# The last transform step of batches 1 to 7: table as weights on 64x32 parts, data streamed, blocks transposed by VectorE

## The chip, the cores and the metric

The kernel runs on one core of a Trainium2 chip. The metric is device time in microseconds (us) for one execution. All times before the change are of this one core; three runs were timed, and one more execution was recorded by the hardware profiler.

The engines are named as in the profile: PE is TensorE (matmuls), PEld its weight loads, DVE is VectorE, ACT is ScalarE, POOL is GpSimd, SP is SyncE (it only issues DMAs here). A matmul takes its weights (`lhsT`) from SBUF, streams the other operand (`rhs`) through the array, and writes a bank of PSUM; there are eight banks. A float32 matmul stands in the trace as two matmul records, with two weight loads.

## The reference

```
x: (8, 3008, 256)                       # batch, sequence, channels
X = rfft(x, axis=1)
y = irfft(X * (filt_r + 1j * filt_i), n=3008, axis=1)
t = y.reshape(24064, 256)
g = t @ w_gate                          # 256 x 1536
out = (g * sigmoid(g) * (t @ w_val)) @ w_out
```

A filter in the frequency domain along the sequence, then a SwiGLU block on every token. Everything is float32.

## The kernel before

The transform of length 3008 = 47 x 64 is done as matrix products with tables of sines and cosines, in steps of length 47 and 64, and the step back as the last of them. The SwiGLU block is done by a scheme with fewer products than the plain one (sums of blocks of inputs and of weights, then products of the sums), with its hidden blocks 0 to 3 and pairs of them.

**Order of the work.** The loop over batches `b` (lines 1431 to 1541) has 12 steps per batch. A step is a `Group(b, k, g)`: one chunk `k` of the tokens (4 chunks of 8 x 94 tokens) and one third `g` of the hidden dimension (`NG = 3`). Each step walks the hand-written list `SCHEDULE` (lines 88 to 96), in which each token stands for one instruction, or a few, on one engine; the order on every engine is this order. `pin` keeps it. A prime on a token means the group before the one it would normally be for. The tokens that matter here:

- `P`, `Q`, `A`, `B`, `E` (`product`, line 1116): two matmuls of 128x128 weights on 188 columns, four records, into a bank.
- `f`, `D`, `c`, `x`, `s`, `y`, `e`, `m`, `l` (`step`, line 1126): copies and sums on ACT, DVE and POOL that fill banks for the products (`s` for `A`, `e` for `E`) or take them out. `g`, `u`: Silu on ACT. `h`, `v`: DVE products into the hidden tiles `h`. `S`: sums of hidden blocks on POOL.
- `W`, `o`, `z`, `x0.o` to `x5.o` (`project`, line 1184): projection matmuls of 376 columns for the group before, their sum into the output tile `o` (line 1234 on DVE; line 1232 on ACT for the first third), the transpose of 32x32 blocks in `o` by DVE (line 1191, only after the last third), and the output DMAs on SP (line 1205). `LAST` (lines 99 to 102) is the order after the last group.
- `b0` to `b7`: pieces of the next batch's transform, `quads` (steps 0 to 3, line 733) and `fours` (steps 4 to 10, line 813). Their matmuls already run on parts of the array, `quads` on 32x32 parts, `fours` on 64x64 parts.
- `t0.0` to `t4.3`: pieces of the last transform step. `plan[step]` (lines 1434 to 1468) lists up to five pieces; `tN.m` advances piece `N`.
- `n1` to `n3`: sums for the next chunk (`combine_sequence`, line 1062).

**The last transform step.** `stage3(k, step)` (line 1008) makes the tile `y` of a chunk from the two halves `t4[k, 0]` and `t4[k, 1]`, each with 2 x 48 rows for each of four row groups `n`. `y` has eight parts of 188 tokens: 0 to 3 from channels 0 to 127 and 4 to 7 from channels 128 to 255, the latter with a multiple (`KS` = -1, 0, 1, 2) of the former taken off. For batch 0 it uses the table `wi_t`. For later batches 4 x 96 rows are packed into three tiles of 128 rows each (`BACK`, lines 120 to 123, loaded by four DMAs, lines 687 to 692); each step is three matmuls with data as weights and the table `back_t` streamed (141, 188 and 141 columns), and the result lands in the order of `y` with tokens of the two tables in turn, written to every second element of the bank (lines 1021 to 1027). Steps with `cb == 0` are taken out by one ACT copy of 376 (line 1041); steps with `cb == 1` by two operations of 188 (lines 1049 to 1054), DVE or ACT, that also take off the multiple.

For batch b its pieces stand so: chunk 1 in steps 0 (t2, t4) and 1 (t1, t3), chunk 2 in step 4 (t0 to t3), chunk 3 in step 7 (t1 to t4), chunk 0 of the next batch in step 11 (t0 to t3). `t4` is loaded two pieces per chunk: for chunks 1, 2, 3 in steps 0, 2 and 5, at the start and at `B01`; for chunk 0 of the next batch in step 10, at `A12` and `E23`.

**Banks.** One bank is in a pool of its own (`fps`, line 240) for `stage1`, `stage2a`, `stage2b` and `stage3`; the other seven (`NB = 7`, line 68) are in the pool `wps` for all else. A tile that is asked for gets a bank whose last readers are done.

Of the kernel before, what the change touches and what calls it, by code (L numbers as in the profile page):

```python
# [66 lines left out]
TQ = TH // 2  # L67
NB = 7

# [29 lines left out]
LAST = """  # L99
S00 S01 W1 S20 S21 S10 S11 W5 o1 W2 o5 S30 S31 W6 o2 z0.o o6 W3 o3 z1.o x0.o x1.o x2.o x3.o x4.o  # L100
x5.o W7 q4 o7 z3.o W4 o4 z2.o X0.o X1.o X2.o X3.o X4.o X5.o
""".split()
# [9 lines left out]
NPR = len(ORDER)  # L112

PIECES = ((0, 7), (7, 14), (14, 20), (20, 26))

BACK = (((0, 0, 0, 48), (1, 48, 0, 48), (2, 96, 0, 32)),  # L120
        ((4, 64, 0, 48), (5, 112, 0, 16), (2, 0, 32, 16), (3, 16, 0, 48)),
        ((5, 0, 16, 32), (6, 32, 0, 48), (7, 80, 0, 48)))
BACK_AT = (0, 3 * N1, 7 * N1)


def dft_tables():
# [12 lines left out]
    one = wi[:, :, 0, :, 0].transpose(1, 0, 2).reshape(2 * NS, N1)  # L139
    back = np.zeros((128, 10 * N1))  # L140
    for tile_, first in zip(BACK, BACK_AT):
        for i, (_, row, a, rows) in enumerate(tile_):
            back[row:row + rows, first + N1 * i:first + N1 * (i + 1)] = one[a:a + rows]


# [15 lines left out]
    one_hi = np.concatenate([np.cos(hi) * scale, -np.sin(hi) * scale * (s > 0)], 1).T  # L161
    for tile_, first in zip(BACK, BACK_AT):
        for i, (n, row, a, rows) in enumerate(tile_):
            if n >= NH:
                back[row:row + rows, first + N1 * i:first + N1 * (i + 1)] = one_hi[a:a + rows]

# [9 lines left out]
    for t in range(NS):  # L176
        u, at = divmod(t, 4)
        for e in range(2):
# [22 lines left out]
    f32 = np.float32  # L201
    return (wf.reshape(NR, NK).astype(f32), wi.reshape(NK, NR).astype(f32),
            back.astype(f32), quad.astype(f32), four.astype(f32), np.ascontiguousarray(de).astype(f32),
# [4 lines left out]
def kernel(  # L208
# [30 lines left out]
    wdpool = pool("wdram", 1, DRAM)  # L239
    fps = pool("fps", 1, PSUM)  # L240
    wps = pool("wps", NB, PSUM)

    wf_t = cpool.tile([NR, NK], FP32)
    wi_t = cpool.tile([NK, NR], FP32)
# [322 lines left out]
    def load_back():  # L567

        t = rpool.tile([128, 2, 128], U32, name="quad", tag="pw", bufs=3)
        t = t.bitcast(FP32).rearrange("p b f -> p (b f)")  # L570
        quad_t.append(t)
        pin(nc.sync.dma_start(out=t[:, 0:65], in_=quad_dram.ap()))
        t = rpool.tile([128, 2, 128, 2], U32, name="back", tag="raw", bufs=2)
        t = t.bitcast(FP32).rearrange("p b f two -> p (b f two)")
        back_t.append(t[:, 0:10 * N1])
        pin(nc.sync.dma_start(out=back_t[0], in_=back_dram.ap()))
# [3 lines left out]
    def bank(name):  # L580
        return wps.tile([128, 512], FP32, name=f"w{name}", tag="w")

    def fbank(name):
        return fps.tile([128, NV, C], FP32, name=name, tag="f")

# [6 lines left out]
    class Spectral:  # L592
# [82 lines left out]
        def load_t4(self, k, i, part=None):  # L675
            at = 2 * k + i
            if part:
                self.load_rows(self.t4[k, i][8 * N_STORED:NK], k, slice(2 * N_STORED, NS), ts(i, NH))
                return
            t = t4pool.tile([128, NH, C], FP32, name=f"t4_{self.b}_{k}_{i}", tag="t4")  # L680
            if part == 0:
                self.load_rows(t[0:8 * N_STORED], k, slice(0, 2 * N_STORED), ts(i, NH), nc.gpsimd)
            elif self.b == 0:
                self.load_rows(t[0:NK], k, slice(0, NS), ts(i, NH))
            else:

                rows = self.d2_tokens.rearrange("(h n) a c -> h (n a) c", h=2)
                rows = rows[:, ts(at, 2 * NS * NH)]
                for j in range(2):
                    self.load(out=t[64 * j:64 * j + 64, 1],  # L690
                              in_=rows[j, 128 * (1 - j):128 * (1 - j) + 64])
                    self.load(out=t[:, 2 * j], in_=rows[j, 64 * j:64 * j + 128])
            self.t4[k, i] = t

        def bank(self, name):

            if self.b == 0:
                return bank(name).rearrange("p (i c) -> p i c", i=NV)
            return fbank(name)

# [200 lines left out]
        def stage1(self, u):  # L901

            t1 = t1pool.tile([NK, NV, C], FP32, name=f"t1_{self.b}_{u}", tag="t1", bufs=2)
            ps = self.bank(f"pa_{self.b}_{u}")
            pin(nc.tensor.matmul(out=ps[0:NK], lhsT=wf_t, rhs=self.x.pop(u),  # L905
                                         start=True, stop=True))
            self.load_x(u + 2)
            yield
            pin(nc.scalar.copy(out=t1, in_=ps[0:NK]))
            pin(nc.scalar.dma_start(out=self.d1_rows[:, ts(u, NV), :], in_=t1))  # L910

        def stage1_first(self, u):


            for cb in range(2):
                ps = bank(f"pa_{u}_{cb}")[:, 0:4 * NK].rearrange("p (n k) -> p n k", k=NK)
                for i in range(4):
                    pin(nc.tensor.matmul(out=ps[:, i], lhsT=x0[u // 2][:, u % 2 * 4 + i, ts(cb, 128)],
                                         rhs=wf_t, start=True, stop=True))
                copy = (nc.scalar.copy, nc.vector.tensor_copy)[cb * (u % 2)]  # L920
# [16 lines left out]
        def stage2a(self, u):  # L937
# [6 lines left out]
            for i in range(NV):  # L944
                pin(nc.tensor.matmul(out=ps[:, i, :], lhsT=self.tb[u][:, i, 0, :],
                                     rhs=t2[:, i, :], start=True, stop=True))
            self.p[u] = pt
# [27 lines left out]
        def stage2b(self, u):  # L975
# [3 lines left out]
            for i in range(NV):  # L979
                pin(nc.tensor.matmul(out=ps[:, i, :], lhsT=tb[:, i, 1, :],  # L980
                                     rhs=pt[:, i, :], start=True, stop=True))
            g = self.place("g", u) if self.b or u < N_TWO - 2 else early("t2", u - 1)
# [25 lines left out]
        def stage3(self, k, step):  # L1008
# [3 lines left out]
            i, cb = divmod(step, 2)  # L1012
            ps = (self.bank if k == 0 else fbank)(f"pd_{self.b}_{k}_{step}")
            psv = ps.rearrange("p a b -> p (a b)")[:, 0:TH].rearrange("p (n r) -> p n r", n=NH)
            flat = ps.rearrange("p a b -> p (a b)")
            back = self.b
            for j in range(len(BACK) if back else 0):
                first = BACK_AT[j]
                cols = back_t[0][:, first:first + N1 * len(BACK[j])]

                if j == 1:
                    rows = flat[:, 1:2 * 187 + 1].rearrange("p (z y) -> p z y", z=2)[:, :, ::2]
                else:
                    at = j // 2 * (2 * N1 + 1)
                    rows = flat[:, at:at + 6 * N1 - 1:2]
                pin(nc.tensor.matmul(out=rows, lhsT=self.t4[k, i][:, j, ts(cb, 128)], rhs=cols,  # L1026
                                     start=j == 0, stop=True, skip_group_check=True))
            for n in range(0 if back else NH):
                pin(nc.tensor.matmul(out=psv[:, n, :],
# [14 lines left out]
            for t in range(2):  # L1044
# [7 lines left out]
                else:  # L1052
                    pin(nc.vector.scalar_tensor_tensor(
                        out=v, in0=b, scalar=-float(k), in1=c, op0=ALU.mult, op1=ALU.add))

# [31 lines left out]
    class Group:  # L1089
# [94 lines left out]
        def project(self, op, last=False):  # L1184
# [3 lines left out]
            if kind == "z":  # L1188
                if q == NG - 1:
                    t = self.part(p)  # L1190
                    pin(nc.vector.transpose(out=t, in_=t))
                return
            if kind in "xXi":
                t, first, count = outs[b, k], 2 * NH * (kind == "X"), 2 * NH if last else 4 * NH
                if kind == "x" and q < NG - 1 and takes_turns(b, k) and p == 5:
                    pin(nc.sync.dma_start(out=o_dram[k], in_=t))
                if q == NG - 1 and (b or kind == "i"):
                    some = (p,) if kind == "i" else (2 * p, 2 * p + 1)
                    for n, (u, cq) in enumerate(divmod(m, 4) for m in some):
                        rows = min(32, NR - 32 * u)  # L1200
                        at = (b * S + 32 * 32 * u + 2 * NH * k) * C + 128 * first + 32 * cq
                        queue = nc.sync if b else nc.gpsimd
                        if last:
                            queue = (nc.sync, nc.scalar, nc.gpsimd)[(2 * p + n) % 3]
                        pin(queue.dma_start(  # L1205
                            out=bass.AP(tensor=out.tensor, offset=out.offset + at,
                                        ap=[[32 * C, rows], [128, count], [1, 32]]),
                            in_=t[32 * cq:32 * cq + rows, first:first + count, ts(u, 32)]))
                return
# [15 lines left out]
            if q == 0 and p == 1:  # L1225
                new_outs(b, k, q)
            i, cb = {1: (0, 0), 2: (0, 0), 6: (0, 1), 3: (0, 1), 4: (1, 0), 7: (1, 1),
                     5: (1, 1)}[p]
            dst = self.part(2 * i + cb)[:, :, 0:NR].rearrange("p n (t r) -> p t n r", t=2)
            src = self.tiles[at].rearrange("p (t n r) -> p t n r", t=2, n=NH)  # L1230
            if q == 0 and at == "A":
# [165 lines left out]


    def chain(*pieces):

# [30 lines left out]
    for b in range(B):  # L1431
# [4 lines left out]
        def three(s, k, cur=cur):  # L1436
            return [s.stage3(k, step) for step in range(4)]

# [15 lines left out]
        if nxt:  # L1454
            gap = iter(())
            plan[0] = [gap, gap, d[0][0], gap, d[0][1]]
            plan[1] = [gap, d[0][2], gap, d[0][3]]
            plan[4], plan[7], plan[11] = d[1], [gap] + d[2], three(nxt, 0)
            if b == 0:
# [7 lines left out]
        else:  # L1467
            plan[1], plan[4], plan[7] = d

# [105 lines left out]
```

## Time and profile before

| what | value |
|---|---|
| median of 3 timed runs | 2806.13 us (2802.09 to 2809.21) |
| span of the profiled execution | 2801.8 us; its whole time is not given apart, so the runs above stand beside it |
| busy: PE, PEld | 2767.8 us (99%), 2308.3 us (82%) |
| busy: DVE, ACT, POOL | 2048.7 us (73%), 1546.7 us (55%), 1579.7 us (56%) |
| matmul records | 15832, of them 672 of the last transform step from batch 1 on |
| DMA | 608.53 MB, mean 217 GB/s |
| granted clock of PE | 0.999 |

The span goes from the first to the last instruction of the profiled execution. A busy time is the union of an engine's instructions. In a group's row, "x448 | 91.0, 284 | 0.0" means 448 records, 91.0 us busy, 284 ns mean of one, and the idle time of the engine just before them. The duration of a matmul record contains the way through the array, and records overlap; the price of a matmul in a dense stretch is the distance between starts. In the timeline a row is the start (us from the span's start), the duration, engine, line, operation, output<-inputs, shapes, count, and in brackets how long the engine was idle before it and what ended that.

The 12 steps of a batch take 27 to 30 us each; batch 1's steps run from about 442 us (step 0) to 780 us. Step 4 of batch 1 starts at 555.1 us, step 5 at 584.95.

### The profile page before, as it was taken

Reading aid. Unit: us, or ns where it says so; the run is one execution under the profiler, and the core shown is the slowest. Engines: PE = TensorE matmul, PEld = TensorE weight load, DVE = VectorE, ACT = ScalarE, POOL = GpSimd, SP = SyncE. Lnnn points to the kernel's source line nnn. Section 1 sums busy time; section 2 is a strip of 40 time slices with the busy share of each in tenths; the row PEclk is TensorE's granted clock in tenths of the full one; section 3 lists DMA queues with packets and bytes.
Section 4 is the critical chain, followed back from the end, with each engine's and each line's share of the span. In section 5 each row is a group of like instructions: output and inputs, shape, how many; then the busy total and the mean of one; then the engine's idle time right before and its main releaser. Section 6 shows DMA issues by size and latency. Waiting matters only on the chain.

```text
span 2801.8 us, 49322 instructions
## 1 busy us (share of the span) xinstructions
PE 2767.8 (99%) x15832; PEld 2308.3 (82%) x15832; DVE 2048.7 (73%) x4675; ACT 1546.7 (55%) x4170; POOL 1579.7 (56%) x1689
## 2 busy tenths in 40 slices
PE   8999999999999999999999999999999999999998
PEld 6777888888888888888888888888888888888887
DVE  7898767776777776777767677777677767666666
ACT  5775445555555555555555555555555555555554
POOL 5886575465545565446554566455555455545544
PEclk9999999999999999999999999999999999999999
DMA  8778877878676776677767776668766677654543
GB/s 216 243 254 285 283 241 238 266 231 268 179 228 207 248 245 190 212 222 232 241 195 219 223 249 218 208 192 262 238 214 197 216 237 233 186 154 145 154 138 83
DMA packets 385272, 608.53 MB, mean 217 GB/s; under 512 B 198876, under 2 KB 268444, under 8 KB 384840
## 3 DMA queue, kind: packets, MB, share of 16 engines
q1 hardware_dynamic: 366202, 574.39, 65.3%
q10 hardware_dynamic: 16174, 25.50, 3.5%
q0 software_dynamic: 2640, 5.51, 0.8%
q8 instruction: 128, 2.10, 0.3%
q14 instruction: 128, 1.05, 0.1%
HBM read 484.65 MB, written 118.12 MB: 215 GB/s over the span
## 4 chain that ended last, share of the span: by engine, by line
PE 90%; POOL 2%; DVE 2%; ACT 1%; issue 1%; DMA 0%; POOLq 0%; ACTq 0%; SPq 0%; DVEq 0%
PE wa L1123 25%; PE wk L1123 17%; PE wA L1220 16%; PE we L1123 12%; PE wG L1220 8%; PE wF L1220 4%; PE pd L1026 3%; PE wqc L823 1%; PE wqb L835 1%; PE wqa L743 1%; POOL h L323 1%; POOL out_dram L1205 0%; PE pa L905 0%; DVE we L323 0%; POOL D L323 0%
## 5 line engine op out<-in xcount | busy, mean ns | idle before, releaser
L1123 PE MATMUL wa<-y_t,wt_t 128*128 128x188 f32 x4464 | 881.0, 323 | 6.5 <-DVE wa L1145 3.4
L1123 PEld LDWEIGHTS wa<-y_t,wt_t 128*128 128x128 f32 x4464 | 745.9, 190 | 88.3 <-ACT wa L1149 11.4
L1123 PEld LDWEIGHTS wk<-y,wt_t 128*128 128x128 f32 x2976 | 493.4, 190 | 113.1 <-issue 37.7
L1123 PE MATMUL wk<-y,wt_t 128*128 128x188 f32 x2976 | 572.8, 325 | 1.7 <-ACT f L1138 1.6
L323 POOL TENSOR_TENSOR h<-h 128x376 f32<-128x376 f32 x572 | 559.3, 998 | 15.1 <-DVE h L320 14.9
L320 POOL TENSOR_TENSOR h<-h 128x376 f32<-128x376 f32 x190 | 182.9, 983 | 673.9 <-DVE h L1170 673.9
L1220 PE MATMUL wA<-h,wo_t 128*128 128x376 f32 x1532 | 548.6, 480 | 4.6 <-DVE o L320 2.1
L1123 PE MATMUL we<-y_t,wt_t 128*128 128x188 f32 x2232 | 431.7, 323 | 1.7 <-ACT we L1154 1.5
L323 POOL TENSOR_TENSOR D<-f,f 128x376 f32<-128x376 f32 x288 | 280.6, 985 | 260.8 <-ACT f L1138 251.6
L323 DVE TENSOR_TENSOR we<-we,m 128x376 f32<-128x376 f32 x576 | 319.6, 556 | 124.8 <-PE we L1123 60.5
L1123 PEld LDWEIGHTS we<-y_t,wt_t 128*128 128x128 f32 x2232 | 369.3, 190 | 2.7 <-ACT we L1154 2.1
L1220 PEld LDWEIGHTS wA<-h,wo_t 128*128 128x128 f32 x1532 | 277.2, 190 | 108.3 <-POOL h L323 5.1
L1158 ACT COPY m<-wa 128x376 f32<-128x376 f32 x576 | 275.1, 478 | 83.1 <-PE wa L1123 78.5
L1165 ACT ACTIVATE u<-we 128x188 f32<-128x188 f32 x576 | 188.6, 327 | 171.8 <-DVE we L323 164.3
L1165 ACT ACTIVATE g<-wa 128x188 f32<-128x188 f32 x576 | 187.3, 326 | 164.6 <-PE wa L1123 157.8
L327 DVE SCALAR_TENSOR_TENSOR y<-wk,c 128x376 f32<-128x376 f32 x480 | 246.6, 540 | 41.4 <-ACT c L1142 24.4
L1220 PE MATMUL wG<-h,wo_t 128*128 128x376 f32 x768 | 274.0, 479 | 0.0
L1142 ACT COPY c<-wk 128x376 f32<-128x376 f32 x288 | 136.9, 475 | 233.1 <-PE wk L1123 232.7
L1154 ACT COPY we<-y 128x376 f32<-128x376 f32 x480 | 222.3, 480 | 19.1 <-DVE h L1170 14.3
L1138 ACT ACTIVATE f<-wk 128x376 f32<-128x376 f32 x288 | 145.0, 504 | 152.6 <-PE wk L1123 115.4
L1170 DVE TENSOR_TENSOR h<-wa,g 128x188 f32<-128x188 f32 x576 | 199.5, 347 | 34.8 <-ACT g L1165 34.6
L1170 DVE TENSOR_TENSOR h<-we,u 128x188 f32<-128x188 f32 x576 | 198.6, 345 | 30.5 <-ACT u L1165 19.2
(195 smaller groups left out, 3563.1 us busy)
## 6 DMA issues: line engine op xcount, KB each, us to landing
wt_t<-w_all SPq DMA_DIRECT2D x174, 896.0 KB
wt_t<-w_all SPq DMA_DIRECT2D x174, 768.0 KB
lent<-filter SPq DMA_DIRECT2D x36, 1024.0 KB
quads<-lent SPq DMA_DIRECT2D x96, 256.0 KB
d<-lent ACTq DMA_DIRECT2D x84, 256.0 KB
lent<-quads SPq DMA_DIRECT2D x144, 128.0 KB
lent<-raw SPq DMA_DIRECT2D x144, 128.0 KB
t<-d SPq DMA_DIRECT2D x114, 128.0 KB
```

Source lines behind the costliest of these rows:

```text
L320: return eng.tensor_tensor(out=dst, in0=a, in1=b, op=ALU.add)
L323: return eng.tensor_tensor(out=dst, in0=a, in1=b, op=ALU.subtract)
L327: return nc.vector.scalar_tensor_tensor(out=dst, in0=a, scalar=-1.0, in1=b, op0=ALU.mult, op1=ALU.subtract)
L1026: pin(nc.tensor.matmul(out=rows, lhsT=self.t4[k, i][:, j, ts(cb, 128)], rhs=cols, start=j == 0, stop=True, skip_group_check=True))
L1123: pin(nc.tensor.matmul(out=ps[:, z], lhsT=self.wt[:, SLOT[p], z], rhs=rhs, start=start and z == 0, stop=True, skip_group_check=True))
L1138: pin(act.mul(self.small(f"f{i}", f"f{i}", 1), t[f"k{i}"], -1.0))
L1142: pin(act.copy(out=self.small(f"c{i}", f"c{i}", 1), in_=t[f"k{i}"]))
L1154: pin(act.copy(out=self.bank(f"e{at}"), in_=t[f"y{at}"]))
L1158: pin(act.copy(out=self.small(f"m{at}", "m", 4), in_=t[f"a{at}"]))
L1165: pin(act.activation(out=self.small(op, "g", 3, 1)[:, 0], in_=ps[:, 1], func=AF.Silu))
L1170: pin(v.tensor_tensor(out=dst, in0=ps[:, 0], in1=g, op=ALU.mult))
L1220: pin(nc.tensor.matmul(out=self.tiles[at], lhsT=wo_t[:, JB * q + i, WO[p], :], rhs=self.hs[i][:, HID[p]], start=start and i == 0, stop=Tru ...
```

## The change

From batch 1 on the last transform step swaps the operands. The table (48 rows, 47 columns, once for each of the two kinds of rows, on partitions 0 to 47 and 64 to 111) becomes the weights, 32 columns at a time, in two goes: columns 0 to 31 (`m = 0`) and 15 to 46 (`m = 1`). The data is streamed, 256 columns a matmul: 32 channels of each of eight runs. A new method `back(k, m)` takes two banks, issues 16 matmuls (2 halves x 4 blocks of 32 channels x 2 kinds), each with 48 rows and 32 output partitions, and then two DVE transposes of 512 that turn 32x32 blocks out of the banks into `y`. After `m = 1` POOL takes off the multiples with four operations of 188. The order of tokens in `y` changes; so the sums into `o` write and read every second element, the transposes of `o` come two at `z1` and two at `z2`, and the last output DMAs go by channel half. `t4` is loaded by two DMAs in place of four. `fps` goes, and `wps` gets eight banks. `wf_t` is padded to 128 columns. `LAST` has another order. The pieces stand in steps 1, 4 and 7 at t2.0 (matmuls), t2.1, t2.2 (transposes) and t3.1, t3.2, t3.3; for chunk 0 of the next batch in step 11 at t0.0 to t0.2 and t2.0 to t2.2. Batch 0 keeps `stage3`, with banks of the pool.

```diff
-NB = 7
+NB = 8
...
 LAST = """
-S00 S01 W1 S20 S21 S10 S11 W5 o1 W2 o5 S30 S31 W6 o2 z0.o o6 W3 o3 z1.o x0.o x1.o x2.o x3.o x4.o
-x5.o W7 q4 o7 z3.o W4 o4 z2.o X0.o X1.o X2.o X3.o X4.o X5.o
+S00 S01 W1 S20 S21 S10 S11 W2 o1 W5 o2 S30 S31 W6 o5 o6 W4 W7 q4 o4 z2.o x0.o x1.o x2.o x3.o x4.o x5.o
+o7 W3 o3 z1.o X0.o X1.o X2.o X3.o X4.o X5.o
...
+LATER = N1 - 32
...
+    back = np.zeros((128, 2, 32))
+    for h, table in enumerate((one, one_hi)):
+        for m in range(2):
+            back[64 * h:64 * h + 2 * NS, m] = table[:, LATER * m:LATER * m + 32]
...
-    fps = pool("fps", 1, PSUM)
...
-                rows = self.d2_tokens.rearrange("(h n) a c -> h (n a) c", h=2)
-                rows = rows[:, ts(at, 2 * NS * NH)]
-                for j in range(2):
-                    self.load(out=t[64 * j:64 * j + 64, 1],
-                              in_=rows[j, 128 * (1 - j):128 * (1 - j) + 64])
-                    self.load(out=t[:, 2 * j], in_=rows[j, 64 * j:64 * j + 128])
+                rows = self.d2_tokens.rearrange("(h n) a c -> h a n c", h=2)
+                for h in range(2):
+                    self.load(out=t[64 * h:64 * h + 2 * NS], in_=rows[h, :, ts(at, NH)])
...
-            for j in range(len(BACK) if back else 0):
...
-                pin(nc.tensor.matmul(out=rows, lhsT=self.t4[k, i][:, j, ts(cb, 128)], rhs=cols,
-                                     start=j == 0, stop=True, skip_group_check=True))
...
+        def back(self, k, m):
+
+            if m == 0:
+                self.y[k] = ypool.tile([128, 8, TQ], FP32, name=f"y_{self.b}_{k}", tag="y")
+            y = self.y[k]
+            banks = [bank(f"pd_{self.b}_{k}_{m}_{h}") for h in range(2)]
+            outs_ = [t.rearrange("p (z i n d) -> p i z n d", z=2, i=2, d=32) for t in banks]
+            for i in range(2):
+                t = self.t4[k, i].rearrange("p n (z j d) -> p j z n d", z=2, d=32)
+                for j in range(4):
+                    for h in range(2):
+                        r = slice(64 * h, 64 * h + 2 * NS)
+                        pin(nc.tensor.matmul(
+                            out=outs_[h][32 * j:32 * j + 32, i], lhsT=back_t[0][r, ts(m, 32)],
+                            rhs=t[r, j], start=i == 0, stop=True, skip_group_check=True))
+            yield
+            to = y.rearrange("p s n -> p (s n)").rearrange("p (z h m r) -> p h z m r", z=2, h=2, r=N1)
+            for h in range(2):
+                pin(nc.vector.transpose(
+                    out=to[:, h, :, :, LATER * m:LATER * m + 32],
+                    in_=banks[h].rearrange("p (z m d) -> p z m d", z=2, d=32)))
+                if h == 0:
+                    yield
+            for a in range(4 if m else 0):
+                b, v = y[:, a], y[:, 4 + a]
+                for _ in range(abs(KS[a])):
+                    pin((sub if KS[a] > 0 else add)(nc.gpsimd, v, v, b))
...
-                    t = self.part(p)
-                    pin(nc.vector.transpose(out=t, in_=t))
+                    for n in ((), (1, 3), (0, 2), ())[p] if b else (p,):
+                        t = self.part(n)
+                        pin(nc.vector.transpose(out=t, in_=t))
...
+            if b:
+                dst = outs[b, k][:, :, 0:NR].rearrange("p (m z) (r h) -> p z h m r", z=2, h=2)[:, cb, i]
+                src = self.tiles[at].rearrange("p (m r) -> p m r", r=N1)
...
+    def later(piece):
+
+        yield
+        yield from piece
...
         def three(s, k, cur=cur):
-            return [s.stage3(k, step) for step in range(4)]
+            if s.b == 0:
+                return [s.stage3(k, step) for step in range(4)]
+            return [s.back(k, m) for m in range(2)]
...
-            plan[0] = [gap, gap, d[0][0], gap, d[0][1]]
-            plan[1] = [gap, d[0][2], gap, d[0][3]]
-            plan[4], plan[7], plan[11] = d[1], [gap] + d[2], three(nxt, 0)
+            first = three(nxt, 0)
+            plan[11] = [first[0], gap, first[1]]
+            if b:
+                plan[1], plan[4], plan[7] = [[gap, gap, p[0], later(p[1])] for p in d]
...
-            plan[1], plan[4], plan[7] = d
+            plan[1], plan[4], plan[7] = [[gap, gap, p[0], later(p[1])] for p in d]
```

## The prediction

> **What bounds the kernel now.** I read the page from the top: busy times, then the chain that ended last, then the costliest groups.
>
> ```profile
> PE 2767.8 (99%) x15832; PEld 2308.3 (82%) x15832; DVE 2048.7 (73%) x4675; ACT 1546.7 (55%) x4170; POOL 1579.7 (56%) x1689
> ...
> PE 90%; POOL 2%; DVE 2%; ACT 1%; issue 1%; DMA 0%; POOLq 0%; ACTq 0%; SPq 0%; DVEq 0%
> ```
>
> The reader is to see that TensorE is busy for 99% of the span and carries 90% of the chain; no other engine has over 2% of it. From batch 1 on (about 407 us) the waits of PE are small: nothing in the list of waits of PE is over 4.8 us in total. So a microsecond of PE time that goes is a microsecond of the kernel, unless another engine is late in its place. What is late next is VectorE, at 73%. The step itself, from the view of groups by shape:
>
> ```profile
> L1026 PE MATMUL pd<-back,t 128*128 128x141 f32 x448 | 91.0, 284 | 0.0
> ...
> L1026 PE MATMUL pd<-back,t 128*128 128x188 f32 x224 | 54.1, 322 | 0.0
> ```
>
> 672 records are 112 steps (7 batches x 4 chunks x 4) of 3 matmuls, two records each. The "mean ns of one" includes the pipeline, so I take prices from starts, in the timeline of PE at two places:
>
> ```profile
> 563.50 0.80 PE L1123 MATMUL wk<-y,wt_t 128*128 128x188 f32 x4
> 564.13 0.96 PE L1026 MATMUL pd<-back,t 128*128 128x141 f32 x6
> 564.93 1.43 PE L1220 MATMUL wA<-h,wo_t 128*128 128x376 f32 x4
> ...
> 1065.56 1.09 PE L823 MATMUL wqc<-lent 64*64 64x256 f32 x16
> 1066.58 1.86 PE L1123 MATMUL wk<-y,wt_t 128*128 128x188 f32 x10
> ...
> 444.57 1.14 PE L743 MATMUL wqa<-lent,quad 24*32 24x512 f32 x32
> 445.64 1.22 PE L1123 MATMUL wk<-y,wt_t 128*128 128x188 f32 x6
> ```
>
> Start to next start is what an item costs: a step of pd 564.93 - 564.13 = 0.80 us (with rounding at both ends 0.808). The other two are bursts on parts of the array: 16 records on 64x64 parts take 1.02, and 32 records of 512 columns on 32x32 parts take 1.07, sixteen of them starting within 0.1 us.
>
> **TensorE: taken away.** 112 steps x 0.808 = 90.5 us.
>
> **TensorE: added.** A call of back() issues 16 matmuls, 32 records of 256 columns, on eight 64x32 parts: four records in line on each part. The trace has no 64x32 part. The 64x64 burst above has the same line (16 records, four parts, four each of 256 columns); the 32x32 burst has the same length in line (two of 512) on sixteen parts. Both pay for going in and out of parts. Going in: the last 376-column record before a burst starts 0.41 before it and should take 0.314, so 0.10 is lost. Coming out: the first 188-column record is followed after 0.26 instead of 0.16, so 0.10. A burst costs 1.02 + 0.20 = 1.23 by the one, 1.07 + 0.20 = 1.27 by the other; I take 1.25. Two calls for each of 28 chunks: 56 x 1.25 = 70.0 us. Net on PE: **-20.5 us**. Bounds: 1.23 gives -21.6. From above, if only four of the eight parts ran at a time, the line would be eight records long, as in the 32-record 64x64 burst: 2.09 with entry and exit, 56 x 2.09 = 117.0, so +26.5. I take the lower end since sixteen parts with four different streams per row group ran side by side in the row. The data is now read in runs of 32 with steps between them; no row of PE reads so, the bound is the same.
>
> One rule speaks of the removed part. The old step writes every second element of its bank; its six records of 141, 188 and 141 columns (940 columns) take 0.804 us, 0.86 ns a column, and contiguous 188-column records start 0.159 apart, 0.85 ns a column. The Trainium skill, "PSUM — Partial Sum Buffer" (Specifications (TRN2)), says that any non-contiguous PSUM pattern slows matmuls significantly; by it the old step should be dear and the change worth more. The row shows nothing of it, and the row decides: nothing is added for it.
>
> **VectorE.** Gone per chunk: one add and two scalar_tensor_tensor of 188 (0.347 + 2 x 0.346 = 1.04); ACT loses two copies of 376 and one of 188 (2 x 0.477 + 0.315 = 1.27). New: four transposes of 512 out of a bank. The nearest rows:
>
> ```profile
> L1191 DVE STREAM_TRANSPOSE o<-o x128: 578/578/581, 300.4 to 2795.9; 128x384 f32<-128x384 f32 x128
> ...
> L853 DVE TENSOR_TENSOR lent<-wqb,lent x72: 680/683/692, 559.0 to 2394.1; 128x512 f32<-128x512 f32 x72
> ...
> L922 DVE COPY lent<-wpa x4: 820/828/876, 10.3 to 24.4; 128x384 f32<-128x384 f32 x4
> ```
>
> 512 elements from a bank take 0.68; the transpose scaled by length gives 0.77. I take 0.69, between 0.58 and 0.83. So +2.76 - 1.04 = +1.7 us per chunk, 48 us in all, beside PE if it fits where it stands. In steps 1, 4 and 7 the second pair stands at t3.2 and t3.3, in the end of the group, where W2 of the next group waits for VectorE's last product. Step 4 of batch 1, VectorE after its add o5:
>
> ```profile
> 580.07 0.55 DVE L320 TENSOR_TENSOR o<-o,wG 128x376 f32<-128x376 f32 x1 [0.83 <-PE wG L1220]
> 580.53 0.35 DVE L1170 TENSOR_TENSOR h<-we,u 128x188 f32<-128x188 f32 x1
> 581.34 1.20 DVE L323 TENSOR_TENSOR we<-we,m 128x376 f32<-128x376 f32 x2 [0.46 <-PE we L1123]
> 582.44 0.84 DVE L1170 TENSOR_TENSOR h<-we,u 128x188 f32<-128x188 f32 x2
> 583.25 0.56 DVE L323 TENSOR_TENSOR we<-we,m 128x376 f32<-128x376 f32 x1
> 583.72 0.34 DVE L1170 TENSOR_TENSOR h<-wa,g 128x188 f32<-128x188 f32 x1
> 584.25 0.35 DVE L1170 TENSOR_TENSOR h<-wa,g 128x188 f32<-128x188 f32 x1 [0.18 <-ACT g L1165]
> 584.52 0.34 DVE L1170 TENSOR_TENSOR h<-we,u 128x188 f32<-128x188 f32 x1
> ```
>
> VectorE is idle 0.46, 0.08, 0.14 and 0.18 here; its last product ends at 584.86 and W2 starts at 585.59, 0.73 later. Two transposes are 1.38; 0.86 falls into the idle time, the last product comes 0.52 later, still inside 0.73. The point from which it costs is (0.73 + 0.86) / 2 = 0.79 us a transpose. The first pair (t2.1, t2.2): the first transpose waits for its burst with everything of VectorE behind it (h01, y23, y03), but PE itself is 1.25 later for all that follows, and VectorE is idle 3.0 us of 571 to 578. Nothing there. Two places are fuller. Step 1 (batches 1 to 6) runs beside quads, and its VectorE is busy 2.5 of 2.5 us from Q3 to A12; there also a pd step at t1.0 goes that covered A01, which PE waits for in steps 0, 2 and 3. Step 11 has the first fold, VectorE busy 4.8 of 4.9 from P2 to Q3. I charge 0.5 us x 6 and 0.4 x 7: **+6 us**, between 0 and 1.4 (both transposes of a pair) per chunk, 39 us.
>
> The o adds and copies now write and read every second element. Reads at that step cost nothing (L430, 0.42 for 256; L327, contiguous, 0.42). Writes of that step are in no row; L922 writes 128 bytes apart and takes 0.83 for 384 where an o add of 376 takes 0.55. So 0 to 0.28 for each of 17 DVE adds per chunk, up to 134 us of VectorE; I take 0, nearest to the read row, which has the same step. The Trainium skill, "SBUF — State Buffer" (Specifications (TRN2), Cachelines), says that a 16-byte line needs two hits: two float32 a line would be free, 128 bytes would not; its sum is 0 as well, and it agrees with L922 at the other end. The z transposes keep their number; two now come together at z1 and z2.
>
> **POOL.** Four operations of 188 at 0.589 = 2.36 us per chunk, 66 us. In steps 1, 4, 7 they follow t3.3, where POOL has been idle over 8 us until the next group's sums (the list of waits has 673.9 us of that, 63 times). In step 11 they come ahead of the sums n2 on POOL, which start about when they end; 0.3 us late at most. If that cover were gone it would be 2.36 per chunk on the next chunk's A products.
>
> **Queues.** t4 loads are two DMAs, not four, each 0.45 to 0.58 of SP. The first burst of step 11 now needs both halves: the second was issued at 746.40 to 748.60, its 1 KB packets ended at 751.5, and the first pd of that step starts at 754.08, so 2.5 us are left (0.7 at batch 0). Nothing. **Banks.** Counting tiles from schedule and last readers, the old pool of 7 has at most 7 alive, the new one 8 of 8, only in steps 1, 4, 7, 11; there e01's bank can come from h12, one instruction earlier, and E01 has 1.65 us of lead. Nothing; other steps gain a bank. **Tail.** Two transposes after the last o3 instead of one: +0.5.
>
> **Sum.** -90.5 + 70.0 + 6 + 0.5 = **-14 us**. The profiled execution has a span of 2801.8; its own whole time is not listed, the runs are 2802.09 to 2809.21, median 2806.13, so some 4 us lie around the span. Span 2788, time **2792**.
>
> **Rivals.**
> 1. VectorE's waits take the place of the matmuls: each back() delays PE 0.4 us, 56 x 0.4 = 22, time 2808, no change. For it: transposes stand in line ahead of products that PE needs, E13 and A23 have only 0.6 to 0.8 us of lead. Against: the idle time counted above. It decides from 0.79 us a transpose.
> 2. Parts: only four of eight run at a time. A burst is 2.09, PE gains 26.5 instead of losing 20.5, time 2806 + 26.5 + 6.5 = 2839, slower. It decides from 90.5 / 56 = 1.62 us a burst. For it: the shape is in no row and its data is strided. Against: sixteen parts side by side in 1.07.
> 3. Strided writes: o adds at 0.83; 1.6 us of VectorE a group. At half of it on PE's path, 67 us less 14, time 2859; at a quarter 2825. It decides once a tenth reaches the path.
> 4. No stall anywhere and the eighth bank helps: 2783 or less.
>
> **Chances.** Forecast, a gain of 8.4 to 23 us: 0.66. Rival 4: 0.04. Rival 1, within 8.4 us: 0.15. Rivals 2 and 3: 0.09 and 0.06. 0.3% of 2806 is 8.4, about what a measurement of this kernel can tell from no change. So faster 0.70, same 0.15, slower 0.15. The range, 2782 to 2806, holds the forecast and most of rival 1.
>
> **What would show it.** After: 1792 records of pd of 256 columns, start to next start 1.02 to 1.07 for 32 of them; transposes from banks at 0.69; o adds still 0.55; PE idle before W2 after steps 4 and 7 as now; POOL's wait before a group shorter by 2.4. A burst over 1.6, a transpose over 0.8 or o adds at 0.6 and more would make the prediction wrong.

## The result, and the profile after

The changed kernel takes **2789.21 us** (median of 4 runs, 2787.99 to 2790.41); the kernel before, run beside it, 2806.53. The ratio is **0.9939**, 95% interval 0.9925 to 0.9953. The prediction said 2792, 2782 to 2806. So the gain is 17.3 us where 14 were forecast.

The page of the changed kernel, busy times and the chain that ended last:

```profile
PE 2748.3 (99%) x16952; PEld 2249.3 (81%) x16952; DVE 2081.7 (75%) x4703; ACT 1514.6 (54%) x4086; POOL 1647.4 (59%) x1801
...
PE 89%; DVE 3%; POOL 2%; ACT 1%; DMA 1%; issue 1%; SPq 0%; POOLq 0%; DVEq 0%; ACTq 0%
```

TensorE still sets the end. It is busy 19.5 us less, VectorE 33 us more, POOL 68 us more, and neither entered the chain by more than a per cent. The groups by shape that carry the change; the first two rows are of the kernel before, the others of the changed kernel:

```profile
L320 DVE TENSOR_TENSOR o<-o,wA 128x376 f32<-128x376 f32 x256 | 138.5, 541 | 26.3 <-PE wA L1220 23.1
L1232 ACT COPY o<-wA 128x376 f32<-128x376 f32 x128 | 61.0, 477 | 106.1 <-PE wA L1220 99.7 <-DMA out_dram<-o 6.0
...
L312 DVE TENSOR_TENSOR o<-o,wA 128x376 f32<-128x376 f32 x256 | 138.8, 542 | 29.5 <-PE wA L1223 28.5
...
L1049 DVE STREAM_TRANSPOSE y<-wpd 128x512 f32<-128x512 f32 x112 | 79.2, 707 | 31.1 <-PE wpd L1043 31.1
L1194 DVE STREAM_TRANSPOSE o<-o 128x384 f32<-128x384 f32 x128 | 67.4, 560 | 2.5
L1239 ACT COPY o<-wA 128x376 f32<-128x376 f32 x128 | 65.3, 510 | 105.4 <-PE wA L1223 103.4 <-DMA out_dram<-o 2.0
```

A transpose of 512 out of a bank takes 0.707 us. The adds into every second element of `o` take 0.542, before 0.541 into neighbours: VectorE writes at that step for nothing. ACT does not: its copy into `o` takes 0.510, before 0.477. Both rows also hold batch 0, which still writes neighbours (16 of the 128 copies, 0.477 each); from batch 1 on a copy takes 0.515, and an add 0.543 beside 0.542 before. A burst, in the timeline of PE (columns as before):

```profile
571.68 0.80 PE L1125 MATMUL wa<-y_t,wt_t 128*128 128x188 f32 x4
572.41 1.09 PE L1043 MATMUL wpd<-t,back 48*32 48x256 f32 x32
573.43 0.91 PE L1125 MATMUL wk<-y,wt_t 128*128 128x188 f32 x4
```

From start to next start it is 573.43 - 572.41 = 1.02 (1.024 with more digits), and entry and exit cost 0.095 and 0.106 in the same places as in the bursts of before: 1.227 us a burst, all but the first of batch 0 (1.41) the same.

**Where the time went.** The profiled execution took 2790.41 us, its span is 2788.6, 13.2 less than before. I cut both spans at the first product of each step. A step's length repeats from batch 2 to 6 within 0.02 us, except step 11:

| stretch | before | after | by the forecast's matmuls alone |
|---|---|---|---|
| start and batch 0 | 442.6 | 448.1 | -0.78 (its step 11) |
| step 0 | 29.17 | 27.57 | -1.62 (two old steps left it) |
| step 1 | 28.48 | 29.11 | +0.84 |
| step 2, step 3 | 27.29, 27.15 | 27.35, 26.75 | 0, 0 |
| step 4, step 7 | 29.83, 30.69 | 29.06, 29.92 | -0.78 each |
| step 11 | 28.60 | 27.8 to 29.3, mean 28.6 | -0.78 |
| steps 5, 6, 8, 9, 10 | | same | 0 |
| batch 1 to the last step's first product | 2316.2 | 2296.1 | -21.0 |
| from there to the end | 43.0 | 44.4 | |

-0.78 is 2 x 1.227 - 4 x 0.808. So steps 4 and 7, 0.77 shorter, give the price of the matmuls and nothing else. Open after this were four things: what cut step 3, why step 11 varies, whether start and batch 0 became slower, and whether the burst, the transposes and POOL have the prices and covers that the forecast gave them.

### The profile page after: what moved, and what is told of

Read it like the earlier page. It is cut to its first block, busy times and chain, and to the rows that moved or that the text cites. A ratio compares the mean times of both kernels' runs of the same rounds, so it can differ in the third digit from the quotient of the medians.

```text
span 2788.6 us, 51410 instructions
## 1 busy us (share of the span) xinstructions
PE 2748.3 (99%) x16952; PEld 2249.3 (81%) x16952; DVE 2081.7 (75%) x4703; ACT 1514.6 (54%) x4086; POOL 1647.4 (59%) x1801
## 3 DMA queue, kind: packets, MB, share of 16 engines
q14 instruction: 127, 1.04, 0.1%
## 4 chain that ended last, share of the span: by engine, by line
PE 89%; DVE 3%; POOL 2%; ACT 1%; DMA 1%; issue 1%; SPq 0%; POOLq 0%; DVEq 0%; ACTq 0%
PE wa L1125 25%; PE wk L1125 17%; PE wA L1223 16%; PE we L1125 12%; PE wG L1223 8%; PE wF L1223 4%; PE wpd L1043 2%; PE wqc L807 1%; PE wqb L819 1%; PE wqa L727 1%; POOL h L315 0%; POOL out_dram L1208 0%; PE wpa L889 0%; DVE we L315 0%; DVE y L319 0%
```

## Experiments

**1 and 2. The eight banks alone.** On the kernel before:

```diff
-NB = 7
+NB = 8
-    fps = pool("fps", 1, PSUM)
-        return fps.tile([128, NV, C], FP32, name=name, tag="f")
+        return bank(name).rearrange("p (i c) -> p i c", i=NV)
```

> The kernel before with one pool of eight banks and nothing else of the change. The forecast held that the banks are worth nothing: then the time is that of before, 2806 us (within 3), and the steps keep their lengths (step 0 29.17, step 2 27.29, step 3 27.15). The rival is that the eighth bank gives what the change gained beyond the forecast: then step 3 becomes 26.75 (-0.4 x 6 = -2.4 us), and step 0 or 2 loses some of the waits of A01 (4.2 us in all in step 0), in sum 2 to 6 us, 2800 to 2804 us.

2806.44 us, ratio 1.0003 (0.9994 to 1.0012). This first kernel leaves out the new start flags of `stage2a` and `stage2b`, on which some sums depend; the number and shape of instructions is the same. The second has them (`start=i == 0` in both):

> The kernel before with one pool of eight banks, as in the first experiment, and with the start flags of the change on the matmuls of stage2a and stage2b (only the first of two regions of a bank clears it). Theory: the banks alone give nothing, 2806 within 3 us, with the steps of the first experiment (step 1 28.27, step 0 29.23, the others within 0.1 of before). Rival, that the flag or the banks carry part of the gain: 2800 to 2803.

2805.56 us, ratio 0.9999 (0.9990 to 1.0009), with step lengths as in the first: step 1 0.21 shorter, steps 0, 2 and 3 longer by 0.06 each. In sum the banks alone are worth nothing, as forecast, but by parts they are not. `Q2`, a product that opens a bank, starts late by 0.13 us in steps 0 to 2 of the kernel before and by 0.19 in step 3, and with eight banks it does not. In steps 0, 2 and 3 `A01`, which waits for a sum of VectorE, then comes 0.27 later than before and eats that up; in step 1 the 0.21 stays. So step 3 needs another cause beside the banks.

**3. The first table narrow again.** On the changed kernel, the pad of `wf` and its 128 columns undone:

```diff
-    wf_t = cpool.tile([NR, 128], FP32)
+    wf_t = cpool.tile([NR, NK], FP32)
```

> The changed kernel with the first table 96 columns wide again, as before. If the wider table is what made the stretch up to the first product of batch 0 4.1 us longer (72.0 to 76.1), the first product starts at 72 and the time is 2785 us. If that stretch varies by itself with the landing of x, the time stays at 2789 (within 2) and the first product can start anywhere from 72 to 77 in the one profile.

2788.51 us (2787.85 to 2789.43), ratio to before 0.9940 (0.9926 to 0.9954): the same as the changed kernel. The first product started at 74.0. Over all profiles here it starts between 69.3 and 78.7, and batch 0 ends between 444.2 and 448.0 in the other versions of the old kernel, where the profile of before had 442.6. So most of the 5.5 us that start and batch 0 lost is spread between executions, not the change; the profile of before was an early one. This is also why the medians differ by more (17.3) than the spans (13.2).

**4. Each transpose out of a bank twice.** On the changed kernel:

```diff
-                pin(nc.vector.transpose(
-                    out=to[:, h, :, :, LATER * m:LATER * m + 32],
-                    in_=banks[h].rearrange("p (z m d) -> p z m d", z=2, d=32)))
+                for _ in range(2):
+                    pin(nc.vector.transpose(out=to[:, h, :, :, LATER * m:LATER * m + 32],
+                                            in_=banks[h].rearrange("p (z m d) -> p z m d", z=2, d=32)))
```

> The changed kernel with each transpose out of a bank issued twice (+112 x 0.708 = 79 us of VectorE). The forecast's window for the second pair of steps 1, 4 and 7 was 0.73 + 0.86 = 1.59 us; the pair takes 1.42, so 0.17 is left, and two more transposes cost 1.25 each of 21 times: +26 us; the first pair and step 11 add between nothing and 1.4 each of 28 times. So 2815 us if only the second pair counts, up to 2855. W2 should then wait for VectorE after steps 1, 4 and 7. The rival, that VectorE is far from the path, gives 2789 to 2793. The other rival, all of it on the path, gives 2868.

2818.13 us in one run, +29: by its size the first theory, but by the steps not. Steps 1, 4 and 7 grew by 0.24 each and the steps after them by 0.22, 0.46 us a chunk where I expected 1.25; step 11 took +1.6 to 2.5 (0.2 in batch 6, which has no fold), the one of batch 0 +3.8. Batches 1 to 7 are 20.0 longer in all; the start and the rest of batch 0, which differ from run to run, have another 4. The second pair in step 4 of batch 1, VectorE in this kernel:

```profile
591.36 0.55 DVE L312 TENSOR_TENSOR o<-o,wG 128x376 f32<-128x376 f32 x1 [2.05 <-PE wG L1223]
591.82 1.46 DVE L1050 STREAM_TRANSPOSE y<-wpd 128x512 f32<-128x512 f32 x2
```

The reader is to see the 2.05 of idle time ahead of `o5`, the same as in the changed kernel; before the change it was 0.83 (the prediction's row). The second burst stands at t3.1, just ahead, and holds TensorE up for 1.2 us while VectorE works off its line. The forecast counted that lead for the first pair and forgot it for the second. So the cover there is about 0.8 deeper than counted. All of the 0.46 stands at products behind the second pair (`E03`, `B03` and, in the next step, `W2`); the first pair costs nothing in steps 1, 4 and 7 even when doubled. Step 11 is the place without cover.

**5. The burst in another order.** All eight matmuls of the first row group, then all eight of the second:

```diff
-            for i in range(2):
-                t = self.t4[k, i].rearrange("p n (z j d) -> p j z n d", z=2, d=32)
-                for j in range(4):
-                    for h in range(2):
+            for h in range(2):
+                for i in range(2):
+                    t = self.t4[k, i].rearrange("p n (z j d) -> p j z n d", z=2, d=32)
+                    for j in range(4):
```

> The changed kernel with the 16 matmuls of a burst in another order: all eight on the first row group, then all eight on the second, so that only four parts have work at a time until the first eight are nearly done. If the side by side of eight parts makes the short burst (1.227 us with entry and exit), the line becomes seven to eight records long (0.213 each): 1.87 to 2.09 a burst, 56 x 0.64 to 0.86 = +36 to +48 us, 2825 to 2837. If PE works off its parts in any order, nothing changes: 2789.

2792.44 us in one run. My theory, +36 to +48, fell: a burst is 1.253, 0.026 more.

```profile
572.23 1.12 PE L1043 MATMUL wpd<-t,back 48*32 48x256 f32 x32
573.28 0.91 PE L1125 MATMUL wk<-y,wt_t 128*128 128x188 f32 x4
```

Single records show four starts from 572.234 on and four more from 572.287 on, and the weight load ahead of these four carries a semaphore wait, as the first load of the second row group does in the changed kernel: the wait for the second bank. So they passed twelve records that stood ahead of them.

**6. Part by part.** A sharper form: both matmuls of a part in a row, then the next part:

```diff
-            for i in range(2):
-                t = self.t4[k, i].rearrange("p n (z j d) -> p j z n d", z=2, d=32)
-                for j in range(4):
-                    for h in range(2):
+            for j in range(4):
+                for h in range(2):
+                    for i in range(2):
+                        t = self.t4[k, i].rearrange("p n (z j d) -> p j z n d", z=2, d=32)
```

> The changed kernel with the 16 matmuls of a burst in a third order: both matmuls of a part one behind the other, then the next part. It settles what the reordered burst of 1.253 us said. Theory: the parts take their work from the issued list on their own, so a matmul whose part is free passes those that wait for another part; then a burst stays within 1.0 to 1.1 us from start to next start (as 1.024 and 1.051 in the other two orders) and the time at 2789 to 2795 us. Rival: matmuls start strictly in the order of issue; then each part's second matmul holds up the seven parts behind it, a burst takes 7 x 2 to 3 records of 0.213 us and a line of 4 and the drain, 4.0 to 5.5 us, and the time is 2789 + 56 x 3.0 to 4.5, 2957 to 3040 us.

2791.14 us in one run, a burst 1.27:

```profile
571.49 1.14 PE L1043 MATMUL wpd<-t,back 48*32 48x256 f32 x32
572.55 0.91 PE L1125 MATMUL wk<-y,wt_t 128*128 128x188 f32 x4
```

In strict order this would have been 4 to 5.5 us, by the estimate above. So the order of issue hardly matters within 16 matmuls. The price fits the work in line on one part, equal on all eight: four records, 4 x 0.213, and 0.17 until the next full-size matmul starts; experiment 7 tries it with eight records. The Trainium skill, "TensorE: Matmul & The Clock Gate" (Part 3, The mechanism), says that matmuls run strictly first in, first out, with only weight loads pulled ahead; these two runs differ from it, and the measurement decides.

**7. The burst twice.** All 16 matmuls of a burst issued again into the same banks:

```diff
-            for i in range(2):
+            for i in (0, 1, 0, 1):
```

> The changed kernel with every burst issued twice in a row, 32 matmuls in place of 16 into the same banks: the line on each part is eight records long, which is the price that the forecast's second rival gave (2.09 us with entry and exit). If TensorE sets the end, a burst grows by 4 x 0.213 = 0.85 us and the time by 56 x 0.85 = 48 us, to 2837 us. If VectorE's transposes or other waits behind the burst set the end, part of it falls into their waits and the time grows by less, 2800 to 2825.

2840.89 us in one run, +51.7. A burst went from 1.024 to 1.888 between starts, 56 x 0.863 = 48.3. In batches 1 to 7 the growth is 44.7: 54 bursts are 46.6, and 2.0 came back as steps 11 became even (30.04 each). TensorE's time passes on in full, and rival 2's burst of 2.09 is what a line of eight records costs (1.888 + 0.20).

**8. One transpose of `o` moved, in the kernel before.** Two at z1, none at z0:

```diff
-                    t = self.part(p)
-                    pin(nc.vector.transpose(out=t, in_=t))
+                    for n in ((), (0, 1), (2,), (3,))[p] if b and not last else (p,):
+                        t = self.part(n)
+                        pin(nc.vector.transpose(out=t, in_=t))
```

> The kernel before with one part of the change alone: the transpose of o that stands at z0 is moved to z1, so that two come together there (but not after the last group). Theory: this, and neither the banks nor the matmuls, took the 0.4 us off step 3, as it stood on VectorE ahead of the sum that A01 waits for. Then step 3 goes from 27.15 to 26.75, step 0 from 29.17 to about 28.9, and the time falls by 3 to 4 us. The forecast's view, that moving the transposes is worth nothing: step 3 stays at 27.15.

2804.69 us beside 2805.17 in one run each, which can't tell 4 us apart; the steps can: step 0 went from 29.17 to 28.58, step 3 from 27.15 to 26.93, 4.3 us in batches 1 to 7. What it does is seen in step 3 of batch 2, VectorE before the change:

```profile
874.71 0.58 DVE L1191 STREAM_TRANSPOSE o<-o 128x384 f32<-128x384 f32 x1
875.21 0.51 DVE L327 SCALAR_TENSOR_TENSOR y<-wk,c 128x376 f32<-128x376 f32 x1
...
875.91 0.55 DVE L1145 SCALAR_TENSOR_TENSOR wa<-wk,D 128x376 f32<-128x376 f32 x1
```

The last line is the sum for A01; it ends at 876.46 and A01 starts at 876.51. The transpose stood in its way. After the change it is gone from there, and A01 starts when TensorE is ready for it. Of step 3's -0.40 this gives 0.22: A01 comes 0.11 earlier and B13 0.10, here and in the changed kernel alike. The other 0.19 is `Q2`, and it goes with the eight banks (experiments 1 and 2); in this run, with seven, it is as late as before. TensorE in the same step, A13 and then Q2, before the change and after it:

```profile
872.96 0.80 PE L1123 MATMUL wa<-y_t,wt_t 128*128 128x188 f32 x4
873.78 0.88 PE L1123 MATMUL wk<-y,wt_t 128*128 128x188 f32 x4
...
874.20 0.80 PE L1125 MATMUL wa<-y_t,wt_t 128*128 128x188 f32 x4
874.84 0.80 PE L1125 MATMUL wk<-y,wt_t 128*128 128x188 f32 x4
```

From start to start it is 0.82 before and 0.64 after. No idle time stands in brackets at 873.78, since the record ahead was still on its way through the array: a list of waits does not show such a delay, the distance between starts does.

**9. The other end of that move.** On the changed kernel, one of the two at z2 moved to z3:

```diff
-                    for n in ((), (1, 3), (0, 2), ())[p] if b else (p,):
+                    for n in ((), (1, 3), (0, 2) if last else (0,), (2,))[p] if b else (p,):
```

> The changed kernel with one of the two transposes of o at z2 moved to z3 (but not after the last group). Theory: the pair at z2 stands on VectorE ahead of the sum that E13 waits for in step 0, where the quads fill VectorE; E13 is 0.43 us late there. Then step 0 goes from 27.57 to 27.15 and 0.4 x 6 = 2.5 us go: 2786 to 2787 us. Rival: the one that is moved makes A03 or E23 late by as much; then the sum of the step stays within 0.1 of 27.57.

2787.56 us in one run, just above the theory's 2786 to 2787; step 0 went from 27.57 to 27.11, the others stayed. VectorE in step 0 of batch 2 of the changed kernel:

```profile
801.03 1.04 DVE L1194 STREAM_TRANSPOSE o<-o 128x384 f32<-128x384 f32 x2
802.00 0.53 DVE L315 TENSOR_TENSOR we<-we,m 128x376 f32<-128x376 f32 x1
802.43 0.55 DVE L319 SCALAR_TENSOR_TENSOR we<-wk,c 128x376 f32<-128x376 f32 x1
```

and with the pair split:

```profile
799.90 0.58 DVE L1194 STREAM_TRANSPOSE o<-o 128x384 f32<-128x384 f32 x1
800.40 0.53 DVE L315 TENSOR_TENSOR we<-we,m 128x376 f32<-128x376 f32 x1
```

The sums behind the pair fill banks for E products. In the changed kernel E13 waits for the second of them, and starts 0.43 later than TensorE could have, of which 0.27 is idle time; in the list of PE's waits (us in total, times, longest):

```profile
PE we L1125 <- DVE we L319: 1.6, 6, 0.3
```

One of the six is in batch 0, the others are the steps 0 of batches 2 to 6. With the pair split it starts on time. So moving the transposes gained at z0 (step 0: 0.59 in the old kernel) and gave 0.46 of it back at z2: "keep their number" was no reason to price them at nothing.

**10. The rows of the batch after next earlier.** On the changed kernel:

```diff
-                if b + 2 < B and (step, op) == (11, "Q0"):
+                if b + 2 < B and (step, op) == (10, "E01"):
```

> The changed kernel with the rows of the batch after next loaded from E01 of step 10 on, and not from Q0 of step 11 on. Theory: in step 11 the first fold waits on VectorE for this transfer (1.2 us in batch 5), and the second transpose of the first pair and the sum for A01 stand behind it; the longer steps 11 (28.3 to 29.3 against 27.84 in batch 6, which has no fold) are made by that. Then all steps 11 come to 27.9 to 28.1 and the one of batch 0 falls by about 1.5: 3 to 5 us in all, 2784 to 2786 us. Rival: the transposes themselves crowd VectorE there; then steps 11 keep their lengths and the time stays at 2789.

2790.76 us in one run, not the 2784 to 2786 of the theory; its batch 0 took 377.0 in place of 372.0. The steps 11 became 28.31 each, from 28.31 to 29.27 (batch 6, which has no fold, kept 27.84): half of the theory, 1.9 us in batches 1 to 7. The changed kernel, step 11 of batch 5:

```profile
2100.58 0.55 DVE L312 TENSOR_TENSOR o<-o,wA 128x376 f32<-128x376 f32 x1 [0.18 <-PE wA L1223]
2102.33 0.69 DVE L312 TENSOR_TENSOR lent<-lent 128x512 f32<-128x512 f32 x1 [1.20 <-DMA lent<-in_x_dram]
2102.94 0.71 DVE L1049 STREAM_TRANSPOSE y<-wpd 128x512 f32<-128x512 f32 x1
...
2105.42 1.51 PE L1125 MATMUL wa<-y_t,wt_t 128*128 128x188 f32 x8 [1.06 <-DVE wa L1147]
```

and with the earlier transfer:

```profile
2101.72 0.55 DVE L312 TENSOR_TENSOR o<-o,wA 128x376 f32<-128x376 f32 x1 [0.18 <-PE wA L1223]
2102.19 1.03 DVE L312 TENSOR_TENSOR lent<-lent 128x512 f32<-128x512 f32 x1
2103.14 0.71 DVE L1049 STREAM_TRANSPOSE y<-wpd 128x512 f32<-128x512 f32 x1
```

The `lent<-lent` sum is the fold, and the PE row is A01, which waits for a sum behind the transpose. The wait of 1.20 for the transfer is gone. The kernel before had this wait too (0.99 in batch 4) and did not feel it; with a transpose behind it, the sum for A01 comes too late. The 28.31 that stay hold another 0.27 of A01. Two things stand ahead of it: the transpose, and the fold itself, which takes 1.03 here in place of 0.69 and so gives 0.33 of the gain back; why it does was not tried.

**11. POOL's multiples thrice.** Taken off, put back, taken off, on the changed kernel:

```diff
-                    pin((sub if KS[a] > 0 else add)(nc.gpsimd, v, v, b))
+                    for f in (sub, add, sub) if KS[a] > 0 else (add, sub, add): pin(f(nc.gpsimd, v, v, b))
```

> The changed kernel with each multiple that POOL takes off taken off, put back and taken off again: 12 operations of 188 in place of 4 per chunk, +8 x 0.6 = 4.8 us of POOL for each of 28 chunks. The forecast said that POOL is idle there and that the multiples are covered. If the cover is deep, steps 1, 4 and 7 and those after them keep their lengths, and only step 11, where the sums n2 stand behind the multiples, can pass some on to step 0: 2789 to 2795 us. If the cover was just enough, the sums of hidden blocks behind them come up to 4.4 us late in each of 21 chunks and the time grows by 50 to 130 us.

2799.57 us in one run, above the 2789 to 2795 of a deep cover, but only +10 for 28 x 4.8 = 134 us of POOL. Steps 1, 4, 7 and 11 kept their lengths; step 2 grew by 0.63, step 0 by 0.42, and in batch 7 steps 2, 5 and 8 by 0.64 each. So where the multiples take 2.4 us, POOL has over 4 us more (4.8 - 0.64) at the end of a chunk before TensorE feels it.

**12. Three moves together.** Experiments 9 and 10, and in step 11 the second transpose of the first pair put off from t0.2 to t0.3, behind the sum for A01:

```diff
-            plan[11] = [first[0], gap, first[1]]
+            plan[11] = [later(first[0], 2), gap, first[1]]
...
-    def later(piece):
+    def later(piece, n=0):
+        for _ in range(n): yield next(piece)
         yield
         yield from piece
```

> The changed kernel with three small moves together: one of the transposes of o from z2 to z3, the rows of the batch after next loaded from E01 of step 10 on, and in step 11 the second transpose of the first pair put off from t0.2 to t0.3, behind the sum that A01 waits for. Theory: from batch 1 to 7 step 0 becomes 27.11 (-0.46 x 6 = -2.8), steps 11 become 27.9 to 28.0 in place of 28.3 to 29.3 (-0.6 x 6 on the mean = -3.6); 2782 to 2784 us, with the interval below the changed kernel's 2788 to 2790. Rival: putting the transpose off only moves the wait to the next sum (E13 or A12 in step 11); then steps 11 stay at 28.3 and the time is 2785 to 2787.

2780.86 us (2776.74 to 2785.38), ratio to before **0.9907** (0.9889 to 0.9926). Steps 11 are 27.96 each (the one of batch 0 too, from 29.82), step 0 is 27.11, the rest is as in the changed kernel; batches 1 to 7 take 2290.1, 6.0 less. Batch 0's step 11 gives 1.9 more in these two profiles, together 7.9 of the 8.3 us between the medians; the profile of this kernel is also an early one (first product at 69.3). The late transpose took the last 0.27 of A01 in step 11, and 0.08 behind it. The times don't touch those of the changed kernel (2787.99 to 2790.41).

## Why the prediction was right, point by point

- **Matmuls removed and added: right.** 0.808 a step and 1.227 a burst (I took 1.25) give 108 x 0.808 - 54 x 1.227 = 21.0 us less in batches 1 to 7 up to the last step; 20.1 were measured. With batch 0's step 11 it is 112 x 0.808 - 56 x 1.227 = 21.8. That eight parts work side by side (against rival 2) is shown by the burst itself, that TensorE's time passes on by experiment 7.
- **Transposes 0.69: 0.71.** Rival 1, decided from 0.79, did not come. The window behind it was worked out too small (experiment 4): the lead that a burst gives to VectorE was left out for the second pair.
- **Stalls +6: near in the two places charged, by luck, and too large in sum.** Step 1, charged 0.5 x 6, had none: it is 0.2 shorter than its matmuls make it, as with eight banks alone. Step 11, charged 0.4 x 7, lost 0.7 on the mean of six (4.2 us) and, in this pair of profiles, 1.5 in batch 0; some 2 us of the 4.2 came by a transfer that the forecast did not look at: the fold that waits for `x` on VectorE. So one place was charged too much and the other too little. The steps 3 gave 2.4 us that were priced at nothing. In sum the stalls in batches 1 to 7 came to about +0.9, and so the gain was larger than -14.
- **The sum.** -21.8 for the matmuls, +0.9 and +1.5 for stalls and +1.4 for the tail make about -18; between the medians it is -17.3.
- **Strided writes: right on VectorE** (0.542 and 0.541), so rival 3 did not come. On ACT 38 ns a copy from batch 1 on, not priced, 4 us of ACT in all; step 10, which holds such copies, kept its 26.62.
- **The transposes of `o`: wrong.** "Keep their number" looked at their sum and not at who waits behind each. The list of PE's waits that the prediction went by shows A01's lateness in step 0 only in part (0.43 of 0.59) and Q2's not at all. The place z0 was worth 0.59 in step 0 and 0.22 in step 3, the pair at z2 cost 0.46.
- **POOL: right**, with a cover deeper than needed. **Banks: nothing by themselves**, as forecast, but not nothing beside the other moves: where the change takes the transpose from ahead of A01, step 3 keeps the 0.19 that Q2 gains by them, and step 1 its 0.21. **`t4` two pieces early: right**, all bursts are alike but the first of batch 0, 0.19 longer; whether its transfer caused that was not tried.
- **Tail: +0.5 priced, +1.4 measured.** From TensorE's last record to the end it is 9.0 us, before 7.0. The last transposes come as a pair, 1.04 against 0.58, and from their end to the end of the span it is 6.10 against 5.33. The order of `LAST` was not tried by itself.
- **Start and batch 0** apart from its step 11 were not priced. They differ by 5.5 us in the two profiles, 0.7 of it in that step; the other profiles show a spread of that size, so the rest is not shown to be the change.

## What to carry to other kernels

Price a matmul burst on parts of the array by the records in line on one part, plus entry and exit, from a burst that is already in the trace; it need not have the same shape. An operation that only moves on an engine's line has a price: ask what stands behind it at the old and at the new place. A wait that cost nothing before the change (here a transfer ahead of the first fold) starts to cost when a new operation stands behind it on the same line; such waits are found by listing what the line already waits for at the places where the change adds something.

## What the runs showed of the hardware that was not expected

Matmuls on different parts of the array pass each other: with 16 of them issued in three orders, among them one that puts each part's work in a row, the burst took 1.227, 1.253 and 1.274 us. VectorE's adds write every second float32 of SBUF at the speed of neighbours (0.542 us for 376), while ACT's copy of the same shape takes 0.515 in place of 0.477 (batch 1 on). What of ACT's 38 ns is the step was not tried apart.
